# A long convolution before two MoE layers: the first half's spectrum stored frequency by frequency, eight complex sums moved to GpSimd

## The chip, the cores and the metric

The kernel runs on one core of a Trainium2 chip. The metric is the device time of one execution in microseconds (us). The engines are TensorE (PE; its weight loads are shown apart as PEld), VectorE (DVE), ScalarE (ACT), GpSimd (POOL) and SyncE (SP), which here only issues DMAs. Each engine works off its own instructions in order and waits for semaphores of the others.

## What is computed

```python
def _attn_ref(x, v, pos_emb, w1, w2):          # S = 12480, D = 128
    h_mlp = np.maximum(pos_emb @ w1, 0.0) @ w2
    window = np.exp(-0.01 * pos)[:, None]
    u = x * v
    Uf = np.fft.rfft(u, n=2 * S, axis=1)
    Hf = np.fft.rfft(h_mlp * window, n=2 * S, axis=0)
    y = np.fft.irfft(Uf * Hf[None, :, :], n=2 * S, axis=1)[:, :S, :]
    return x * y
# then two MoE layers, 128 -> 2048 -> 128:
# relu(h)^2 and max(h, 0) + alpha * min(h, 0)
```

All operands are float32. The convolution is a multiplication of spectra, over a transform of length 110 x 229 that is done as two smaller ones (a over 110, b over 229), each a set of matmuls with tables of cosines and sines.

## The kernel before

The 128 channels are worked on in two halves of 64 (h = 0, 1). A stage is a Python generator that yields after each step; `run((gen, n), ...)` interleaves generators, advancing each by 1/n per step, and so fixes the order on every engine. The stages around the change are, with their place in the profile:

1. **First transforms** (44.6 to 115.3 us). `u_stage(0)` transforms the first half in 16 steps of four channels (`u_mm_a3`, then `u_mm_b3`), while `r_stage` makes the filter's tiles r. In `u_mm_b3` two DVE operations (line 301) write the even and the odd sums, 448 elements each, into the spectrum's place U(0, ...).
2. **Second transforms with first products** (115.3 to 188.9). `u_stage(1)` does the second half (`u_mm_a`, `u_mm_b`, DVE line 325). `p_stage(0)` multiplies the first half's spectrum by the filter's: 14 items, each for four frequencies. An item has two halves. In a half PE makes the filter's spectrum H in a PSUM bank (line 368: four matmuls, shown as 8 records), and DVE multiplies it with the spectrum into tile A (named T) or B (named wide) (line 373). Then DVE subtracts and adds A and B (line 382, two operations of 512 elements), and `finish` on GpSimd writes sums and differences back over the spectrum (line 352). The last item of all finishes on DVE. Two PSUM banks (ring r_h) hold H.
3. **Second products with first inverse** (200.7 to 250.8). `p_stage(1)` does the same for the second half, while `b_stage(0)` does the inverse b transform of the first half: 16 steps of 8 matmuls (line 391, 16 records a step), whose lhsT is one cell of the spectrum, its 112 values (2 x 56 frequencies); ACT copies the result out (line 399).
4. **Second inverse** (250.8 to 277.7), with the decoding of MoE weights, then the inverse a transform with the output product (`y_stage`, lines 444 and 445, to 333), then the MoE layers to the end.

GpSimd also prepares the input (`prep`, lines 271 and 210), some steps ahead of the transform that reads it; SP loads it (`load`). xv_ring has NV = 10 pairs of buffers for it. The first half's spectrum lies in gaps of the large buffer G, whose rows are 256 floats apart: cell x is a row, and its 112 values are neighbours. The first XF = 16 cells lie in one set of gaps, the rest in another, so that each operation over all cells comes in two parts.

Of the kernel before, what the change touches and what calls it, by code (L numbers as in the profile page):

```python
# [9 lines left out]
F32 = mybir.dt.float32  # L10
# [3 lines left out]
I64 = mybir.dt.int64  # L14
# [7 lines left out]
KA = HA + 1  # L22
# [5 lines left out]
KP = KA // 2  # L28
XF = 16
NAP = -(-NA // 16) * 16  # L30
DH = D // 2
DG = 4
# [26 lines left out]
def kernel(  # L59
# [70 lines left out]

    def U(h, x0, n):
        if h:
            return R2[:HB].rearrange("p (x k) -> p x k", k=K2)[:, x0:x0 + n]
        if x0 < XF:
            return gap[0][:HB, x0:x0 + n, 128 - K2:128]
        return gap[1][:HB, x0 - XF:x0 - XF + n, 0:K2]

    def parts(h):
        return [(0, D)] if h else [(0, XF), (XF, D - XF)]

    NV = 10
    at = [XF]

    def rows(n):
        at[0] += n
        assert at[0] <= HX
        return gap[0][:, at[0] - n:at[0]]

    a_ring = [[rows(DG)[:, :, 0:K2] for _ in range(2)] for _ in range(2)]
    t_ring = [rows(DG)[:, :, 0:K2] if i else gap[1][:, D - XF:D - XF + DG, 0:K2] for i in range(2)]  # L150
    n_old = -(-(HP - at[0]) // DG)
# [137 lines left out]
    def u_mm_b3(k):  # L289
        hi, lo = a_t.pop(k)  # L290
        ps = [bank(r_b, HB, 2, DG, KA) for _ in range(2)]
        t = t_ring[k % 2][:HB].rearrange("p d (c k) -> p c d k", c=2)
        for eo in (1, 0):
            th, tl = (tab[:, eo] for tab in df3)
            for i, (w, x) in enumerate(((th, lo), (tl, hi), (th, hi))):
                nc.tensor.matmul(ps[eo], lhsT=w, rhs=x[:, eo], start=i == 0, stop=i == 2)
            if eo:
                nc.scalar.copy(out=t, in_=ps[1])
        u = U(0, 2 * DG * k, 2 * DG).rearrange("p (d s) (c k) -> p s c d k", s=2, c=2)
        for s, op in enumerate((ALU.add, ALU.subtract)):  # L300
            nc.vector.tensor_tensor(out=u[:, s], in0=ps[0], in1=t, op=op)

# [9 lines left out]
    def u_mm_b(k):  # L312
        h, g = divmod(k, NG)
        a = a_t.pop(k)
        pe = bank(r_b, HB, DG, 2, KA)
        po = bank(r_b, HB, DG, 2, KA)
        nc.tensor.matmul(po[:, :, 0], lhsT=sinb, rhs=a[0][:, :, 1])
        nc.tensor.matmul(pe[:, :, 0], lhsT=cosb, rhs=a[0][:, :, 0])
        nc.tensor.matmul(po[:, :, 1], lhsT=sinb, rhs=a[1][:, :, 0])
        t = t_ring[k % 2][:HB].rearrange("p d (c k) -> p d c k", c=2)  # L320
        nc.scalar.copy(out=t, in_=po)
        nc.tensor.matmul(pe[:, :, 1], lhsT=cosb, rhs=a[1][:, :, 1])
        u = U(h, 2 * DG * g, 2 * DG).rearrange("p (d s) (c k) -> p d s c k", s=2, c=2)
        for s, op in enumerate((ALU.add, ALU.subtract)):
            nc.vector.tensor_tensor(out=u[:, :, s], in0=pe, in1=t, op=op)

    def u_stage(h, parts=None):
        for k in range(h * NG, (h + 1) * NG + 1):
            if k < (h + 1) * NG:
                prep(k + NV - 4)  # L330
                load(k + NV - 1)
                u_mm_a3(k, parts) if parts else u_mm_a(k)
                yield
            if k > h * NG:
                u_mm_b3(k - 1) if parts else u_mm_b(k - 1)
                yield
# [3 lines left out]
    p_order += [(j + nj - 6) % nj for j in range(nj)]  # L340

    def p_stage(h, t_ring, r_ring):
        def at_j(x0, m, j):
            return U(h, x0, m).rearrange("p x (c k) -> p x c k", c=2)[:, :, :, 4 * j:4 * j + 4]

        def finish(n, j, A):
            eng = nc.vector if n == 2 * nj - 1 else nc.gpsimd
            for x0, m in parts(h):
                y = A[:, x0:x0 + m].rearrange("p (d s) c k -> p d s c k", s=2)
                u = at_j(x0, m, j).rearrange("p (d s) c k -> p d s c k", s=2)  # L350
                for s, op in ((0, ALU.add), (1, ALU.subtract)):
                    eng.tensor_tensor(out=u[:, :, s], in0=y[:, :, 0], in1=y[:, :, 1], op=op)

        for n in range(h * nj, (h + 1) * nj):
            j = p_order[n]
            m = p_order[min(n + 2, 2 * nj - 1)]
            if m not in r_t:
                del r_t[p_order[n - 1]]
                r_t[m] = r_ring()
                nc.sync.dma_start(out=r_t[m].rearrange("p q c k -> p (q c k)"), in_=spill[m])  # L360
            r = r_t[j]
            A = t_ring()
            B = wide[:HB].rearrange("p (x c k) -> p x c k", k=4, c=2)
            for c, out_c in enumerate((A, B)):
                H = bank(r_h, HB, DH, 2, 2, 2)
                for q in range(2):
                    for s in range(2):
                        nc.tensor.matmul(
                            H[:, :, s, q], lhsT=r[:, q, 2 * s + c], rhs=w2_sb[:, h * D:(h + 1) * D]
                        )  # L370
                hv = H.rearrange("p d s q r -> p (d s) (q r)")
                for x0, m in parts(h):
                    nc.vector.tensor_tensor(
                        out=out_c[:, x0:x0 + m],
                        in0=at_j(x0, m, j),
                        in1=hv[:, x0:x0 + m].unsqueeze(2).to_broadcast([HB, m, 2, 4]),
                        op=ALU.mult,
                    )
                if c == 0:
                    yield  # L380
            for c, op in ((0, ALU.subtract), (1, ALU.add)):
                nc.vector.tensor_tensor(out=A[:, :, c], in0=A[:, :, c], in1=B[:, :, 1 - c], op=op)
            finish(n, j, A)
            yield

    def b_stage(h, alone):
        for g in range(NG):
            for e in range(2):
                p = bank(r_y if alone else r_ab, K2, DG, HX)
                for d in range(DG):  # L390
                    nc.tensor.matmul(
                        p[:, d], lhsT=U(h, 2 * (g * DG + d) + e, 1)[:, 0], rhs=icosb if e == 0 else isinb
                    )
# [103 lines left out]
    def weights(pool, n=2):  # L497
        s_ring = ring_of(pool, 3, [128, n, 128], I64, "s_w")
        rings = [ring_of(pool, 2, [128, n * 128], F32, t) for t in ("f_w", "m_w")]

# [35 lines left out]

        return go

# [178 lines left out]
    with tc.manual_schedule():  # L717
        with ExitStack() as st:
# [17 lines left out]
            wst = ctx.enter_context(tc.tile_pool(name="wst", bufs=1))  # L736
            decode = weights(wst)
            back = decode([
# [7 lines left out]
            big = st.enter_context(tc.tile_pool(name="tt", bufs=1, side="right"))  # L746
            tt = ring_of(big, 2, [HB, D, 2, 4], F32, "T")
            p0, q0 = p_stage(0, tt, r_ring), p_stage(1, tt, r_ring)
            run((u_stage(1), 2 * NG), (p0, 2 * nj - 4))
            next(back)  # L750
            for _ in range(3):
                next(q0)
            run((q0, 2 * nj + 3), (b_stage(0, False), NG))
        banks = six + last_two("pair", 512, 512)
        r_y.items = six
        wa = ctx.enter_context(tc.tile_pool(name="wa", bufs=1))
        w["i0"] = [(wa.tile([128, 2, NT, 128], F32R, name="w_i0"), 0, NT)]
# [173 lines left out]
```

## Time and profile before

| what | value |
|---|---|
| median of 3 runs | 1404.55 us (1404.37 to 1404.98) |
| profiled execution | 1402.77 us of device time, span of its core 1401.0 us |
| PE busy | 1389.3 us, 99% |
| DVE, ACT, POOL busy | 1158.4, 977.8, 1006.9 us |
| mean granted PE clock | 0.998 of 2.4 GHz |

A busy share of PE counts its records from start to end, and records of successive matmuls overlap; how fast PE really goes is read from the starts of successive records. Stages are told apart by their windows, and what ends a wait stands in brackets behind a row of the timeline.

### The profile page before, as it was taken

To read this page: it belongs to the slowest core of one execution; us is meant where nothing else is said; L and a number is where in the kernel's file an instruction comes from. 1 tells how busy PE (TensorE), PEld (TensorE's weight loads), DVE (VectorE), ACT (ScalarE), POOL (GpSimd) and SP (SyncE) were. 2 spreads that over 40 slices of the span, in tenths; PEclk is the share of its full clock that TensorE was granted. 3 is DMA by queue.
4 is the path that set the end of the run, shared out by engine and by line. 5 is a ranking of instruction groups with operands and counts; after the bars stand their busy time and mean duration, and the time that the engine had idled before them with its cause. 6 is when DMAs were issued, how large, how long until landed. Compare 5 with 4: busy or idle time off the path is not lost.

```text
span 1401.0 us, 22648 instructions
## 1 busy us (share of the span) xinstructions
PE 1389.3 (99%) x7566; PEld 1205.7 (86%) x7566; DVE 1158.4 (83%) x1824; ACT 977.8 (70%) x1850; POOL 1006.9 (72%) x841
## 2 busy tenths in 40 slices
PE   9999999999999999999999999999999999999998
PEld 9999989998888888888888888888888888888898
DVE  5688899786888888888888888788888878888888
ACT  4454322725988778778777877877787787777777
POOL 4954856446787777877777777777777777777777
PEclk9999999999999999999999999999999999999999
DMA  7565323397000000000000000000000000000000
GB/s 209 173 200 177 94 82 109 105 275 218 24 16 1 8 1 9 8 8 8 9 8 0 9 8 9 8 8 8 8 2 8 8 9 8 9 8 1 8 9 19
DMA packets 59016, 66.20 MB, mean 47 GB/s; under 512 B 6226, under 2 KB 48019, under 8 KB 58771
## 3 DMA queue, kind: packets, MB, share of 16 engines
q1 hardware_dynamic: 57802, 60.62, 14.3%
q0 software_dynamic: 688, 3.93, 0.8%
q8 instruction: 59, 0.97, 0.3%
q14 instruction: 58, 0.48, 0.1%
q10 hardware_dynamic: 409, 0.21, 0.1%
HBM read 47.83 MB, written 16.92 MB: 46 GB/s over the span
## 4 chain that ended last, share of the span: by engine, by line
PE 79%; ACT 1%; POOL 1%; DVE 1%; issue 0%; POOLq 0%; DVEq 0%
PE bank L605 19%; PE bank L607 19%; PE bank L606 19%; PE pair L606 6%; PE pair L607 6%; PE pair L605 6%; PE bank L444 2%; PE bank L445 2%; ACT G L399 1%; POOL g L658 1%; ACT pair L517 0%; ACT w_i L487 0%; DVE pair L477 0%; DVE f_w L481 0%; DVE pair L475 0%
## 5 line engine op out<-in xcount | busy, mean ns | idle before, releaser
L658 POOL TENSOR_TENSOR g<-R,g 128x512 fp32r<-128x512 f32 (+1 forms) x601 | 779.4, 1314 | 253.5 <-ACT g L647 241.3
L640 DVE SCALAR_TENSOR_TENSOR R<-bank,e 128x512 f32<-128x512 f32 (+1 forms) x800 | 530.1, 672 | 137.4 <-POOL g L658 99.8
L647 ACT CAST g<-R 128x512 fp32r<-128x512 f32 (+1 forms) x800 | 469.8, 605 | 77.5 <-DVE R L640 70.0
L625 ACT ACTIVATE e<-bank 128x512 f32<-128x512 f32 (+1 forms) x400 | 235.0, 587 | 106.6 <-PE bank L607 104.6
L630 DVE TENSOR_SCALAR e<-bank,alpha 128x512 f32<-128x512 f32 (+1 forms) x266 | 195.0, 733 | 36.0 <-PE bank L607 34.4
L658 DVE TENSOR_TENSOR g<-R,g 128x512 fp32r<-128x512 f32 (+1 forms) x199 | 184.7, 928 | 0.0
L606 PE MATMUL pair<-g,w_o 128*128 128x512 f32 (+1 forms) x400 | 153.7, 384 | 0.4 <-POOL g L658 0.4
L605 PE MATMUL bank<-x,w_i 128*128 128x512 f32 (+1 forms) x400 | 153.8, 384 | 0.0
L605 PE MATMUL pair<-g,w_o 128*128 128x512 f32 (+1 forms) x400 | 153.6, 384 | 0.0
L606 PE MATMUL bank<-x,w_i 128*128 128x512 f32 (+1 forms) x400 | 153.6, 384 | 0.0
L607 PE MATMUL bank<-x,w_i 128*128 128x512 f32 (+1 forms) x400 | 153.5, 384 | 0.0
L607 PE MATMUL pair<-g,w_o 128*128 128x512 f32 (+1 forms) x400 | 153.5, 384 | 0.0
L605 PE MATMUL bank<-g,w_o0b 128*128 128x512 f32 (+1 forms) x350 | 134.4, 384 | 0.0
L606 PE MATMUL bank<-g,w_o0b 128*128 128x512 f32 (+1 forms) x350 | 134.3, 384 | 0.0
L607 PE MATMUL bank<-g,w_o0b 128*128 128x512 f32 (+1 forms) x350 | 134.3, 384 | 0.0
L627 ACT ACTIVATE e<-bank 128x512 f32<-128x512 f32 (+1 forms) x134 | 78.7, 588 | 33.5 <-PE bank L607 32.9
L628 ACT ACTIVATE e<-e,alpha 128x512 f32<-128x512 f32 (+1 forms) x134 | 95.5, 713 | 4.4
L605 PEld LDWEIGHTS bank<-x,w_i 128*128 128x128 f32 x400 | 75.1, 188 | 15.0 <-DVE R L640 0.9
L606 PEld LDWEIGHTS pair<-g,w_o 128*128 128x128 f32 x400 | 75.2, 188 | 14.8 <-POOL g L658 1.0
L607 PEld LDWEIGHTS bank<-x,w_i 128*128 128x128 f32 x400 | 75.1, 188 | 14.4
L607 PEld LDWEIGHTS pair<-g,w_o 128*128 128x128 f32 x400 | 75.1, 188 | 14.4
L606 PEld LDWEIGHTS bank<-x,w_i 128*128 128x128 f32 x400 | 75.2, 188 | 13.8
(137 smaller groups left out, 2526.0 us busy)
## 6 DMA issues: line engine op xcount, KB each, us to landing
r<-spill SPq DMA_DIRECT2D x22, 460.0 KB, 3.2
G<-in_xs_dram SPq DMA_DIRECT2D x32, 224.0 KB, 3.5
G<-in_vs_dram SPq DMA_DIRECT2D x32, 224.0 KB, 3.5
spill<-r SPq DMA_DIRECT2D x14, 460.0 KB, 3.0
out_dram<-R SPq DMA_DIRECT2D x23, 256.0 KB, 2.0
R<-in_xt_dram SPq DMA_DIRECT2D x27, 218.0 KB, 4.2
s_w<-in_moe_w_in_dram SPq DMA_DIRECT2D x16, 256.0 KB, 3.6
s_w<-in_moe_w_out_dram SPq DMA_DIRECT2D x16, 256.0 KB, 2.7
```

Source lines behind the costliest of these rows:

```text
L444: nc.tensor.matmul(pv, lhsT=le, rhs=re, start=True, stop=False)
L445: nc.tensor.matmul(pv, lhsT=lo, rhs=ro, start=False, stop=True)
L605: nc.tensor.matmul(p, lhsT=wl, rhs=xh, start=first, stop=False)
L606: nc.tensor.matmul(p, lhsT=wh, rhs=xl, start=False, stop=False)
L607: nc.tensor.matmul(p, lhsT=wh, rhs=xh, start=False, stop=last)
L625: nc.scalar.activation(out=r, in_=p, func=ACTF.Relu)
L627: nc.scalar.activation(out=r, in_=p, func=ACTF.Relu, scale=-1.0)
L628: nc.scalar.activation(out=r, in_=r, func=ACTF.Copy, scale=alpha[:, t:t + 1])
L630: nc.vector.tensor_scalar(out=r, in0=p, scalar1=0.0, scalar2=alpha[:, t:t + 1], op0=ALU.min, op1=ALU.mult)
L640: nc.vector.scalar_tensor_tensor(out=g, in0=p, scalar=0.0, in1=r, op0=ALU.max, op1=op)
L647: nc.scalar.copy(out=gh, in_=g)
L658: eng.tensor_tensor(out=gl, in0=g, in1=gh.bitcast(F32), op=ALU.subtract)
```

## The change

The first half's spectrum is turned: a row of the gap now holds one of the 112 values (a frequency, real or imaginary) for all 128 cells, `u0[p, c, k, s, d]`, with the d index running through neighbours; one value of the next frequency lies 256 floats, that is 1,024 bytes, further. All of it fits one set of gaps, so the split in two parts goes. `u_mm_b3` writes it with k as the innermost loop; `b_stage` takes a column of it as lhsT (`u_cells`). In the first products tiles A and B are laid out in the same way, and H is written into its bank with an order (q r s d) in place of (d s q r).

For the 8 items n of `on_pool`, of 28, GpSimd does the two sums of line 382 too; B of such an item is a tile of the T ring, which has three tiles in place of two. The space comes from two gaps that become free and from the decoding of weights, whose later tiles are now set up after the products. xv_ring has 12 pairs, so signals are loaded two steps earlier; they are prepared as far ahead as before. The pace of `p_stage(0)` is 29 steps in place of 24, against the transforms' 32, and two steps of the second products follow in place of three.

```diff
     gap = [G.rearrange("p (n h x) -> p n h x", h=2, x=128)[:, :, h] for h in range(2)]
 
-    def U(h, x0, n):
+    u0 = gap[1][:HB, :K2].rearrange("p (c k) (s d) -> p c k s d", c=2, s=2)
+    u1 = R2[:HB].rearrange("p (d s c k) -> p d s c k", s=2, c=2, k=KA)
+
+    def u_cells(h, d, e):
         if h:
-            return R2[:HB].rearrange("p (x k) -> p x k", k=K2)[:, x0:x0 + n]
-        if x0 < XF:
-            return gap[0][:HB, x0:x0 + n, 128 - K2:128]
-        return gap[1][:HB, x0 - XF:x0 - XF + n, 0:K2]
-
-    def parts(h):
-        return [(0, D)] if h else [(0, XF), (XF, D - XF)]
-
-    NV = 10
-    at = [XF]
+            return u1[:, d, e].rearrange("p c k -> p (c k)")
+        return gap[1][:HB, :K2, e * DH + d]
+
+    NV = 12
+    at = [0]
...
                 nc.tensor.matmul(ps[eo], lhsT=w, rhs=x[:, eo], start=i == 0, stop=i == 2)
             if eo:
                 nc.scalar.copy(out=t, in_=ps[1])
-        u = U(0, 2 * DG * k, 2 * DG).rearrange("p (d s) (c k) -> p s c d k", s=2, c=2)
         for s, op in enumerate((ALU.add, ALU.subtract)):
-            nc.vector.tensor_tensor(out=u[:, s], in0=ps[0], in1=t, op=op)
+            u = u0[:, :, :, s, DG * k:DG * (k + 1)].rearrange("p c k d -> p c d k")
+            nc.vector.tensor_tensor(out=u, in0=ps[0], in1=t, op=op)
 
     def u_mm_a(k):
...
@@ -320,14 +317,13 @@
         t = t_ring[k % 2][:HB].rearrange("p d (c k) -> p d c k", c=2)
         nc.scalar.copy(out=t, in_=po)
         nc.tensor.matmul(pe[:, :, 1], lhsT=cosb, rhs=a[1][:, :, 1])
-        u = U(h, 2 * DG * g, 2 * DG).rearrange("p (d s) (c k) -> p d s c k", s=2, c=2)
         for s, op in enumerate((ALU.add, ALU.subtract)):
-            nc.vector.tensor_tensor(out=u[:, :, s], in0=pe, in1=t, op=op)
+            nc.vector.tensor_tensor(out=u1[:, DG * g:DG * (g + 1), s], in0=pe, in1=t, op=op)
 
     def u_stage(h, parts=None):
         for k in range(h * NG, (h + 1) * NG + 1):
             if k < (h + 1) * NG:
-                prep(k + NV - 4)
+                prep(k + NV - 6)
                 load(k + NV - 1)
...
+    on_pool = {1, 4, 7, 10, 15, 18, 21, 24}
+
     def p_stage(h, t_ring, r_ring):
-        def at_j(x0, m, j):
-            return U(h, x0, m).rearrange("p x (c k) -> p x c k", c=2)[:, :, :, 4 * j:4 * j + 4]
+        def shaped(t):
+            if h:
+                return t.rearrange("p (d s c k) -> p c (d s) k", s=2, c=2, k=4)
+            return t.rearrange("p (c k x) -> p c k x", c=2, k=4)
+
+        def at_j(j):
+            k = slice(4 * j, 4 * j + 4)
+            if h:
+                return u1[:, :, :, :, k].rearrange("p d s c k -> p c (d s) k")
+            return u0[:, :, k].rearrange("p c k s d -> p c k (s d)")
 
         def finish(n, j, A):
             eng = nc.vector if n == 2 * nj - 1 else nc.gpsimd
-            for x0, m in parts(h):
-                y = A[:, x0:x0 + m].rearrange("p (d s) c k -> p d s c k", s=2)
-                u = at_j(x0, m, j).rearrange("p (d s) c k -> p d s c k", s=2)
-                for s, op in ((0, ALU.add), (1, ALU.subtract)):
-                    eng.tensor_tensor(out=u[:, :, s], in0=y[:, :, 0], in1=y[:, :, 1], op=op)
+            if h:
+                y, u = A.rearrange("p (d s z) -> p s d z", s=2, z=8), u1[:, :, :, :, 4 * j:4 * j + 4]
+                u = [u[:, :, s] for s in range(2)]
+            else:
+                y = A.rearrange("p (z s d) -> p s z d", s=2, z=8)
+                u = [u0[:, :, 4 * j:4 * j + 4, s] for s in range(2)]
+            for s, op in ((0, ALU.add), (1, ALU.subtract)):
+                eng.tensor_tensor(out=u[s], in0=y[:, 0], in1=y[:, 1], op=op)
 
...
+            apart = n in on_pool
+            B = t_ring() if apart else wide[:HB]
             A = t_ring()
-            B = wide[:HB].rearrange("p (x c k) -> p x c k", k=4, c=2)
             for c, out_c in enumerate((A, B)):
-                H = bank(r_h, HB, DH, 2, 2, 2)
+                H = r_h()[:HB].rearrange("p (d s q r) -> p s q d r" if h else "p (q r s d) -> p s q d r", s=2, q=2, r=2)
                 for q in range(2):
                     for s in range(2):
-                        nc.tensor.matmul(
-                            H[:, :, s, q], lhsT=r[:, q, 2 * s + c], rhs=w2_sb[:, h * D:(h + 1) * D]
-                        )
-                hv = H.rearrange("p d s q r -> p (d s) (q r)")
-                for x0, m in parts(h):
-                    nc.vector.tensor_tensor(
-                        out=out_c[:, x0:x0 + m],
-                        in0=at_j(x0, m, j),
-                        in1=hv[:, x0:x0 + m].unsqueeze(2).to_broadcast([HB, m, 2, 4]),
-                        op=ALU.mult,
-                    )
+                        nc.tensor.matmul(H[:, s, q], lhsT=r[:, q, 2 * s + c], rhs=w2_sb[:, h * D:(h + 1) * D])
+                hv = H.rearrange("p s q d r -> p (d s) (q r)" if h else "p s q d r -> p (q r) (s d)")
+                o, u = shaped(out_c), at_j(j)
+                if h:
+                    o, u = (x.rearrange("p c x k -> p x c k") for x in (o, u))
+                    hv = hv.unsqueeze(2).to_broadcast([HB, D, 2, 4])
+                else:
+                    hv = hv.unsqueeze(1).to_broadcast([HB, 2, 4, D])
+                nc.vector.tensor_tensor(out=o, in0=u, in1=hv, op=ALU.mult)
                 if c == 0:
                     yield
+            a, b = shaped(A), shaped(B)
             for c, op in ((0, ALU.subtract), (1, ALU.add)):
-                nc.vector.tensor_tensor(out=A[:, :, c], in0=A[:, :, c], in1=B[:, :, 1 - c], op=op)
+                eng = nc.gpsimd if apart else nc.vector
+                eng.tensor_tensor(out=a[:, c], in0=a[:, c], in1=b[:, 1 - c], op=op)
             finish(n, j, A)
             yield
...
                 for d in range(DG):
                     nc.tensor.matmul(
-                        p[:, d], lhsT=U(h, 2 * (g * DG + d) + e, 1)[:, 0], rhs=icosb if e == 0 else isinb
+                        p[:, d], lhsT=u_cells(h, g * DG + d, e), rhs=icosb if e == 0 else isinb
                     )
                 dst = gv[:, :, e, h * DH + g * DG:h * DH + (g + 1) * DG]
...
@@ -744,15 +758,18 @@
             (wide,) = last_two("wide", 1024)
             r_b.items, r_h.items, r_ab.items = six[2:4], six[4:6], six[0:4]
             big = st.enter_context(tc.tile_pool(name="tt", bufs=1, side="right"))
-            tt = ring_of(big, 2, [HB, D, 2, 4], F32, "T")
+            tt = ring_of(big, 2, [HB, D * 8], F32, "T")
+            third = st.enter_context(tc.tile_pool(name="third", bufs=1))
+            tt.items.append(third.tile([HB, D * 8], F32, name="T2"))
             p0, q0 = p_stage(0, tt, r_ring), p_stage(1, tt, r_ring)
-            run((u_stage(1), 2 * NG), (p0, 2 * nj - 4))
+            run((u_stage(1), 2 * NG), (p0, 2 * nj + 1))
             next(back)
-            for _ in range(3):
+            for _ in range(2):
```


On PE this is the end of the second transforms and the beginning of the first inverse. L314 to L322 are transforms, L368 (before) and L378 (after) halves of products, L391 and L401 the inverse. First before, then of the changed kernel:

```order
L319 MATMUL bank_72<-G,dfb 115x4x56
L322 MATMUL bank_71<-G,dfb 115x4x56
L368 MATMUL bank_73<-w_sb,r_100 115x64x2 x4
L368 MATMUL bank_74<-w_sb,r_100 115x64x2 x4
L368 MATMUL bank_73<-w_sb,r_98 115x64x2 x4
L368 MATMUL bank_74<-w_sb,r_98 115x64x2 x4
L368 MATMUL bank_73<-w_sb,r_99 115x64x2 x4
L368 MATMUL bank_74<-w_sb,r_99 115x64x2 x4
L368 MATMUL bank_73<-w_sb,r_100 115x64x2 x4
L368 MATMUL bank_74<-w_sb,r_100 115x64x2 x4
L391 MATMUL bank_69<-dfb,G 112x116 x4
```


```order
L314 MATMUL bank_72<-G,dfb 115x4x56
L315 MATMUL bank_71<-G,dfb 115x4x56
L316 MATMUL bank_72<-G,dfb 115x4x56
L319 MATMUL bank_71<-G,dfb 115x4x56
L378 MATMUL bank_73<-w_sb,r_99 115x64x2 x4
L378 MATMUL bank_74<-w_sb,r_99 115x64x2 x4
L378 MATMUL bank_73<-w_sb,r_100 115x64x2 x4
L401 MATMUL bank_69<-dfb,G 112x116 x4
```


Eight halves of products stood between the last transform and the inverse, and three do now; the five others have moved ahead, between the transforms.

On DVE this is a stretch of the first products among the second transforms (L325, L321), before and after; T and wide are the tiles A and B, G the spectrum:

```order
L325 TENSOR_TENSOR R_82<-bank_71,G 115x4x112 x2
L373 TENSOR_TENSOR T_1089<-G,bank_73 115x128
L373 TENSOR_TENSOR T_1089<-G,bank_73 115x896
L373 TENSOR_TENSOR wide_1084<-G,bank_74 115x128
L373 TENSOR_TENSOR wide_1084<-G,bank_74 115x896
L382 TENSOR_TENSOR T_1089<-T_1089,wide_1084 115x128x4 x2
L325 TENSOR_TENSOR R_82<-bank_71,G 115x4x112 x2
L373 TENSOR_TENSOR T_1088<-G,bank_73 115x128
L373 TENSOR_TENSOR T_1088<-G,bank_73 115x896
L325 TENSOR_TENSOR R_82<-bank_71,G 115x4x112 x2
```


```order
L386 TENSOR_TENSOR T_1088<-G,bank_73 115x1024
L386 TENSOR_TENSOR wide_1083<-G,bank_74 115x1024
L392 TENSOR_TENSOR T_1088<-T_1088,wide_1083 115x512 x2
L321 TENSOR_TENSOR R_82<-bank_71,G 115x4x112 x2
L386 TENSOR_TENSOR T_1087<-G,bank_73 115x1024
L386 TENSOR_TENSOR T_1092<-G,bank_74 115x1024
L321 TENSOR_TENSOR R_82<-bank_71,G 115x4x112 x2
L386 TENSOR_TENSOR T_1088<-G,bank_73 115x1024
L321 TENSOR_TENSOR R_82<-bank_71,G 115x4x112 x2
L386 TENSOR_TENSOR wide_1083<-G,bank_74 115x1024
```


Each product is one instruction in place of two, and an item on GpSimd (its B in a T tile too) has no sums (L382, L392) behind its products. On GpSimd the sums stand in front of that item's `finish`, between two preparations (L268, L207):

```order
L361 TENSOR_TENSOR G<-T_1087 115x2x4x64 x2
L268 TENSOR_TENSOR G<-G 110x4x115
L207 TENSOR_TENSOR G<-G,sig_sb 110x4x115
L392 TENSOR_TENSOR T_1092<-T_1092,T_1088 115x512 x2
L361 TENSOR_TENSOR G<-T_1092 115x2x4x64 x2
```


## Rows read from the trace of the kernel before

**Rows 1.** Windows by stage: length, busy per engine (records), clock, DMA, GB/s

```profile
core 0: us, PE busy (x) PEld busy (x) DVE busy (x) ACT busy (x) POOL busy (x), PEclk, DMA share, GB/s
44.60:115.30 70.70, 70.26 (x578) 67.72 (x577) 57.81 (x120) 35.34 (x77) 45.19 (x39) 1.00 0.64 192
115.30:188.90 73.60, 73.34 (x594) 71.49 (x592) 64.04 (x106) 25.87 (x49) 49.10 (x62) 1.00 0.42 129
188.90:200.70 11.80, 8.88 (x50) 8.02 (x50) 11.56 (x18) 0.00 (x0) 7.86 (x11) 0.71 0.12 39
200.70:250.80 50.10, 49.12 (x451) 47.02 (x450) 48.27 (x55) 16.93 (x31) 32.29 (x26) 1.00 0.35 103
```

**Rows 2.** Timeline of PE, one step: start, length (us), line, records

```profile
176.12 1.77 PE L309 MATMUL bank<-dfa,G 110*115 110x112 f32 x16
...
179.25 1.04 PE L368 MATMUL bank<-w_sb,r 128*115 128x128 f32 x8
180.12 1.77 PE L309 MATMUL bank<-dfa,G 110*115 110x112 f32 x16
```

**Rows 3.** Timeline of PE at the hand-over, [idle before <- releaser]

```profile
187.03 1.91 PE L368 MATMUL bank<-w_sb,r 128*115 128x128 f32 x16
190.71 1.13 PE L368 MATMUL bank<-w_sb,r 128*115 128x128 f32 x8 [1.77 <-DVE T L373]
...
194.56 6.28 PE L368 MATMUL bank<-w_sb,r 128*115 128x128 f32 x32 [0.91 <-DVE T L373]
200.68 1.75 PE L391 MATMUL bank<-dfb,G 115*112 115x116 f32 x16
```

**Rows 4.** Timeline of PE, second products with first inverse

```profile
217.87 1.75 PE L391 MATMUL bank<-dfb,G 115*112 115x116 f32 x16
219.46 2.17 PE L368 MATMUL bank<-w_sb,r 128*115 128x128 f32 x16
...
225.24 1.75 PE L391 MATMUL bank<-dfb,G 115*112 115x116 f32 x16
```

**Rows 5.** Lines of DVE by form, 40 to 255: busy, mean ns, idle before

```profile
L382 DVE TENSOR_TENSOR T<-T,wide 115x512 f32<-115x512 f32 x56 | 36.0, 683 | 1.0
L301 DVE TENSOR_TENSOR G<-bank,G 115x448 f32<-115x448 f32 x32 | 18.5, 619 | 3.6 <-PE bank L296 2.8 <-ACT G L298 0.5
L373 DVE TENSOR_TENSOR wide<-R,bank 115x1024 f32<-115x1024 f32 x14 | 17.2, 1226 | 0.7 <-PE bank L368 0.2
L373 DVE TENSOR_TENSOR T<-R,bank 115x1024 f32<-115x1024 f32 x14 | 17.0, 1212 | 0.0
L373 DVE TENSOR_TENSOR wide<-G,bank 115x896 f32<-115x896 f32 x14 | 15.3, 1095 | 0.5
L373 DVE TENSOR_TENSOR wide<-G,bank 115x128 f32<-115x128 f32 x14 | 4.0, 289 | 3.6 <-PE bank L368 3.6
```

**Rows 6.** Lines of POOL by form, same stretch

```profile
L352 POOL TENSOR_TENSOR R<-T 115x512 f32<-115x512 f32 x26 | 32.3, 1264 | 15.5 <-DVE T L382 15.5
```

**Rows 7.** Source line 197: ns min/median/max, first and last start, forms

```profile
L197 DVE SCALAR_TENSOR_TENSOR G<-bank,win_sb x9: 262/1056/1073, 5.6 to 17.7; 110x512 f32<-110x512 f32 x7, 110x256 f32<-110x256 f32 x1, 110x64 f32<-110x64 f32 x1
```

**Rows 8.** Timeline of PE, last steps of the first transforms

```profile
114.14 0.47 PE L296 MATMUL bank<-xl,df 115*115 115x448 f32 x1 [0.44 <-DVE G L301]
```

**Rows 9.** Timeline of PE's weight loads, two stretches

```profile
110.44 0.97 PEld L242 LDWEIGHTS pair<-dfb,R 115*128 115x128 f32 x8
...
278.89 0.31 PEld L445 LDWEIGHTS bank<-ido,G 112*128 112x128 f32 x2
279.13 0.31 PEld L444 LDWEIGHTS bank<-ide,G 112*128 112x128 f32 x2
279.37 0.31 PEld L445 LDWEIGHTS bank<-ido,G 112*128 112x128 f32 x2
```

**Rows 10.** Timeline of PE in the MoE layers

```profile
799.73 0.39 PE L605 MATMUL bank<-x,w_i 128*128 128x512 f32 x1
...
802.90 0.39 PE L607 MATMUL bank<-x,w_i 128*128 128x512 f32 x1
```

More of the change, by code (lines that the diff above doesn't have):

```diff
@@ L28 @@
 KP = KA // 2
-XF = 16
 NAP = -(-NA // 16) * 16
@@ L149 @@
     a_ring = [[rows(DG)[:, :, 0:K2] for _ in range(2)] for _ in range(2)]
-    t_ring = [rows(DG)[:, :, 0:K2] if i else gap[1][:, D - XF:D - XF + DG, 0:K2] for i in range(2)]
+    t_ring = [rows(DG)[:, :, 0:K2] if i else gap[1][:, K2:K2 + DG, 0:K2] for i in range(2)]
     n_old = -(-(HP - at[0]) // DG)
@@ L312, in u_mm_b @@
     def u_mm_b(k):
-        h, g = divmod(k, NG)
+        g = k - NG
         a = a_t.pop(k)
@@ L497, in weights, with more @@
     def weights(pool, n=2):
-        s_ring = ring_of(pool, 3, [128, n, 128], I64, "s_w")
-        rings = [ring_of(pool, 2, [128, n * 128], F32, t) for t in ("f_w", "m_w")]
+        s_ring = ring_of(pool, 2, [128, n, 128], I64, "s_w")
+        rings = []
+        def more(pool):
+            s_ring.items.append(pool.tile([128, n, 128], I64, name="s_w2"))
+            rings.extend(ring_of(pool, 2, [128, n * 128], F32, t) for t in ("f_w", "m_w"))
         def go(todo):
@@ L535, in go @@
                     yield
-        return go
+        return go, more
     def in_place(key):
@@ L736 @@
             wst = ctx.enter_context(tc.tile_pool(name="wst", bufs=1))
-            decode = weights(wst)
+            decode, more = weights(wst)
             back = decode([
@@ L755 @@
         r_y.items = six
+        more(ctx.enter_context(tc.tile_pool(name="wst2", bufs=1)))
         wa = ctx.enter_context(tc.tile_pool(name="wa", bufs=1))
```

## Prediction

> **What bounds the kernel now.** I read the windows by stage first [rows 1], then PE's timeline inside each, then the groups of instructions by shape. In both transform stages and in the second products TensorE (PE) shows 98% busy or more, so a busy share does not separate them; the pace does. In the second transform stage PE repeats a cycle without gaps [rows 2]: the transforms of one step run from 176.12 to 179.25, 3.13 us, and a half of products (8 records of line 368) from 179.25 to 180.12, 0.87 us. From 115.3 to the last transform's end at 187.03 there are 16 steps and 23 halves: 16 x 3.13 + 23 x 0.87 = 70.1 of 71.7 us. That stage is PE's, and only 1.6 us of it is stall.
>
> Then comes a gap [rows 3]: from 187.03 to 200.68, 13.65 us, PE has only 8 halves, 7.0 us of work at that pace. It waits for VectorE's (DVE's) products, and the granted clock falls: 0.71 over 188.9 to 200.7 [rows 1], that is, partly the lower level of 1.2 GHz. So 6.65 us are lost. In the stage after it two products and two inverse steps repeat every 7.37 us (217.87 to 225.24) [rows 4]. PE's own work in that is 2 x 1.59 for 32 inverse records (16 from 217.87 to 219.46, so 99 ns each) and 4 x 0.87 for products: 6.66. DVE, busy 48.27 of 50.1 us [rows 1], sets this period. Over the stage PE has 24 halves (20.9) and 256 inverse records (25.4): 46.3 of 50.1, 3.8 us lost.
>
> All that the change can win on PE's side is thus 1.6 + 6.65 + 3.8 = 12 us, 0.9% of the time. What follows (second inverse, outputs, both MoE layers) starts when the first inverse ends, so a shift of that end (250.8) moves the kernel's end one for one.
>
> **What it takes off.** *DVE.* Each first-half product is one instruction of 1,024 elements in place of 128 + 896. The second half has that size already: 1,226 ns against 289 + 1,095 for tile B [rows 5]. That is 0.16 us a product, 4.4 us over 28. Eight items give their two sums of 683 ns to GpSimd: 10.9 us in all, half in each stage. In the second stage DVE then has at most 14 x 2.44 for products, 10 x 1.37 for sums and 32 x 0.62 for line 325 (the shape of line 301): 67.7 us under PE's 74.5 (below). In the third it has 14 x 2.44 + 10 x 1.37 = 47.9.
>
> *GpSimd.* It gets 16 sums; the nearest row is its own 512-element operation at 1,264 ns [rows 6]: 10 us a stage. It was busy 49.1 of 73.6 us in the second stage [rows 1] and gets 5 more for two finishing items that fell behind it: 64 of 75. It is fullest while it still prepares signals; the third tile gives DVE about two items (over 10 us) before a tile comes back, so I take 0 and keep 1 us of stall for the range. The signal loads that move ahead on SP's queue keep their distance to the preparations: nothing, since DMA is 42% busy there.
>
> *The hand-over.* The order shows 3 halves behind the last transform in place of 8. PE's work ahead of that point is 16 x 3.13 + 28 x 0.87 = 74.5, with the stalls of today 76.1. After it PE fills two banks (1.75 us) and needs the first one back. DVE still has one product, two sums, two line-325 pairs and the next product behind it, some 6.1 us after PE's last first-half product, against 3.1 + 1.75 on PE: 1.3 us of waiting, then 0.87 for the third half. The inverse's first matmul also waits for GpSimd's last finish (2 x 1.26 after DVE's sums), which is over by then.
>
> **What it adds.** *Writes of line 301.* They now step through 1,024 bytes between elements (frequency is the inner loop). The only strided writer of today is line 197, 920 bytes apart: 512 elements take 1,056 ns, 64 take 262 [rows 7], so 1.772 ns an element and 149 fixed. For 448 that makes 943 in place of 619 ns [rows 5]: 32 x 0.324 = 10.4 us more on DVE in the first stage, where it is busy 57.8 of 70.7 and PE 70.3 [rows 1]. It still fits (68.2), and a freed bank is wanted only a step later, except at the end, where PE already waits for this line [rows 8]: the last pair is 0.65 us longer. I take 0.65; ends 0 (the writes cost as now) and 3 (DVE's queue becomes the bound).
>
> *Weight loads of the first inverse.* This is the term that decides. Its 256 records take as lhsT one column of the frequency rows: 112 elements 1,024 bytes apart, where they were neighbours. The records now follow at 99 ns, which is what their 116 moving columns need (128 of line 368 take 0.87 / 8 = 109), so any longer load shows in full. No row has such a load. From below: line 444 loads 128 columns 8 bytes apart, line 242 128 neighbours; two loads of 444/445 take 0.235 us (278.89, 279.13, 279.37), 118 ns each, while 8 of line 242 take 0.97 with 0.19 for the last, 111 each [rows 9]. So a small stride already costs some 7 ns, and below that nothing: 99. From above: line 197's price for a lone element, 1.772 ns [rows 7]. I take it, because the 8-byte row sits where it puts that load: if 1.772 is the price of one access that can bring two such neighbours, 64 x 1.772 = 113 of the 118 are explained and 5 are a fixed part; a load that pays by columns alone would have shown 111. Lone columns then make 112 x 1.772 + 5 = 204 ns.
>
> The Trainium skill (SBUF — State Buffer, section Door 1: The DMA port swizzle) says that SBUF has lines of 16 bytes, and that each access that crosses into a new line pays. The trace agrees: MoE matmuls read 512 neighbours, 128 such lines, and start 226 ns apart (14 in 3.17 us) [rows 10], which is 128 x 1.77. By that page too a load of 112 lone columns would be an estimated 198 ns and more, with the sum as below.
>
> **Sum**, in the profiled execution's time (span 1401.0, device time 1402.77; the runs' median is 1404.55, 1.78 above). First stage +0.65. Last transform ends at 115.3 + 0.65 + 76.1 = 192.1; with 1.75 + 1.3 + 0.87 the inverse starts at 196.0 in place of 200.7: -4.7, the 0.65 included. Third stage: 25 halves x 0.87 + 256 x 0.204 = 21.8 + 52.2 = 74.0 in place of 50.1: +23.9; DVE's 47.9 lies under it. Together +19.2: 1422.0 in the profile's terms, **1424** as a median.
>
> **Rivals.**
> 1. *Strided loads are free* (the other side). The third stage is then 21.8 + 25.4 = 47.2, DVE about equal, 1 us of stall: 48.2, -1.9; with -4.7 that is -6.6: **1398**. For it: DVE's price is of writes, and a read may be fetched ahead; against it: the 118 of rows 9. It decides below 99 + 6.6/256 = 125 ns a record; above that the kernel is slower. The Trainium skill (TensorE: Matmul & The Clock Gate, section LDWEIGHTS) counts a load by columns alone, columns / 1.2; by that estimate 112 need 93 ns at any stride and this rival holds. The trace speaks against it with 118 and 111 for the same 128 columns.
> 2. *The clock falls.* With loads of 204 ns the array streams under half of the time of an inverse record. Today the granted clock fell after 188.94 to 192.05, when PE ran one half, and the 32 records from 194.56 took 6.1 us in place of 3.5 [rows 3]. At the lower level a half costs 0.87 more; if half of the 25 do: +11, **1435**; all: 1446. Against it: products, dense, stand between the inverse steps.
> 3. *First products slow down in PSUM.* Line 368 now writes neighbours in order 512 bytes apart; today it writes pairs 32 bytes apart, at the same 109 ns a record as its 128 columns need [rows 2], so nothing is the near end. If lone words cost as on line 197 (1.7 times), 28 x 0.87 x 0.7 = 17 us: **1441**. The same section of the skill gives PSUM lines of 8 bytes and says that matmuls slow down on patterns that are not contiguous; today's pairs fill such a line, which is why no row tests it.
>
> **How the numbers follow.** Forecast 0.76, rival 1 0.13, rival 2 0.06, rival 3 0.05. The low end, 1411, is a load halfway between its ends (151 ns, 256 x 0.052 = 13.4 us over rival 1); the high end, 1438, takes in half of the clock's case and 3 us for line 301. Outside lie rival 1 and most of rival 3. No change means within 0.2% (2.8 us), about what a measurement of this kernel can tell: faster 0.12, same 0.02, slower 0.86.
>
> **What will show it.** PEld of the first inverse: 204 ns from start to start against 99, with no DVE wait between; line 301 at 943 ns; the inverse starting at 196 and ending at 270. Right on the other parts and wrong on the sum would be: inverse records still at 99 and an end at 244 (rival 1), a granted clock under 1 after 196 (rival 2), halves longer than 0.87 between 115 and 192 (rival 3). A T tile waited for by DVE on GpSimd would show the third tile too small.

## The result, and the profile after

The changed kernel takes 1421.93 us (median of 4 runs, 1420.35 to 1422.32), the kernel before 1404.46 (4 runs, 1402.86 to 1404.98). The ratio is 1.0125, 95% interval 1.0113 to 1.0138: 17.5 us slower. The profiled execution took 1420.35 us, with a span of 1418.6.

The windows by stage of the changed kernel, cut where its stages change (first transforms, second transforms with first products, hand-over, second products with first inverse, second inverse):

```profile
core 0: us, PE busy (x) PEld busy (x) DVE busy (x) ACT busy (x) POOL busy (x), PEclk, DMA share, GB/s
44.60:116.00 71.40, 70.44 (x579) 67.90 (x578) 62.83 (x120) 35.52 (x78) 45.15 (x39) 1.00 0.64 191
116.00:192.80 76.80, 75.24 (x610) 73.15 (x609) 63.88 (x80) 25.50 (x49) 62.90 (x52) 1.00 0.37 111
192.80:197.30 4.50, 4.50 (x27) 4.28 (x25) 3.31 (x4) 0.35 (x1) 0.17 (x1) 0.66 0.02 4
197.30:268.10 70.80, 70.80 (x458) 70.80 (x456) 45.11 (x49) 16.94 (x31) 42.37 (x34) 1.00 0.27 79
268.10:295.20 27.10, 25.71 (x259) 25.53 (x258) 21.47 (x51) 21.86 (x53) 14.60 (x20) 1.00 0.36 100
```

Against [rows 1] the inverse starts at 197.3 in place of 200.7, a gain of 3.4 us. The next stage then takes 70.8 us in place of 50.1. DVE, which was its limit with 48.27 us of 50.1, is now busy 45.11 of 70.8; PE and its weight loads fill the window. Behind it nothing changes: the second inverse takes 27.1 us (26.9 before), and the rest follows 17.5 us later than before.

PE's timeline in that stage (start, length, line, records), which answers to [rows 4]:

```profile
228.33 1.91 PE L378 MATMUL bank<-w_sb,r 128*115 128x128 f32 x16
230.08 3.24 PE L401 MATMUL bank<-dfb,G 115*112 115x116 f32 x16
233.15 1.91 PE L378 MATMUL bank<-w_sb,r 128*115 128x128 f32 x16
```

Sixteen records of the inverse run from 230.08 to 233.15, 3.07 us or 192 ns each, where they took 99. Sixteen of the product take 1.75 us, 109 ns each, as before. No row has an idle time in front. The source view of the inverse's line (first inverse from G, second from R) has the cause on the weight loads: durations min/median/max in ns, first and last start.

```profile
L401 PEld LDWEIGHTS bank<-dfb,G x256: 264/287/288, 197.2 to 267.9; 115*112 115x112 f32 x128
...
L401 PEld LDWEIGHTS bank<-dfb,R x256: 177/177/192, 268.1 to 293.4; 115*112 115x112 f32 x128
```

The same 115 x 112 load takes 110 ns longer from start to end where its columns lie 1,024 bytes apart; loads overlap, so from start to start it is 93 (192 against 99). The line that writes the turned spectrum (301 before, 298 now) and DVE's products by form, with the idle time before them and what ended it:

```profile
L298 DVE TENSOR_TENSOR G<-bank,G 115x448 f32<-115x448 f32 x32 | 27.8, 945 | 3.5 <-PE bank L293 2.7 <-ACT G L295 0.5
...
L386 DVE TENSOR_TENSOR T<-G,bank 115x1024 f32<-115x1024 f32 x18 | 21.8, 1215 | 6.1 <-POOL G L361 3.9 <-POOL G L268 1.2 <-PE bank L378 0.7
```

945 ns in place of 619 [rows 5]. At the end of the first transforms PE waits longer for that line (answers to [rows 8]):

```profile
114.82 0.46 PE L293 MATMUL bank<-xl,df 115*115 115x448 f32 x1 [0.96 <-DVE G L298]
```

The row of line 386 has a wait that was not there: DVE stands 5.1 us for GpSimd before its products. At the hand-over (answers to [rows 3]) PE's timeline is:

```profile
191.52 0.64 PE L315 MATMUL bank<-G,dfb 115*115 115x224 f32 x2 [1.27 <-DVE R L321]
...
193.02 4.41 PE L378 MATMUL bank<-w_sb,r 128*115 128x128 f32 x24
197.27 3.03 PE L401 MATMUL bank<-dfb,G 115*112 115x116 f32 x15
```

Three halves, 24 records, take 4.25 us to the inverse's start, 2.6 at the full clock: the granted clock was 0.66 in that window.

### The profile page after: what moved, and what is told of

It reads as the page before. It is cut to its first block, busy times and chain, and to the rows that moved or that the text cites. A ratio compares the mean times of both kernels' runs of the same rounds, so it can differ in the third digit from the quotient of the medians.

```text
span 1418.6 us, 22573 instructions
## 1 busy us (share of the span) xinstructions
PE 1408.8 (99%) x7566; PEld 1227.6 (87%) x7566; DVE 1153.0 (81%) x1780; ACT 978.2 (69%) x1850; POOL 1023.1 (72%) x829
## 4 chain that ended last, share of the span: by engine, by line
PE 78%; ACT 1%; POOL 1%; DVE 1%; issue 0%; POOLq 0%; DVEq 0%
PE bank L619 19%; PE bank L620 19%; PE bank L621 19%; PE pair L620 6%; PE pair L619 6%; PE pair L621 6%; PE bank L454 2%; PE bank L455 2%; ACT G L409 1%; POOL g L672 1%; ACT pair L531 0%; ACT w_i L497 0%; DVE pair L487 0%; DVE f_w L491 0%; DVE pair L485 0%
```

## The experiments

The theory behind all of them: the loss is the lone columns of the first inverse's weight loads (columns without a neighbour that is read too), and a load pays for each group of 16 bytes that it touches. The rivals: the turned layout costs elsewhere (writes, PSUM, clock), or the price has another form. A second question came with the numbers: which part of the change brings the 3.4 us, and what it would bring without the loads.

**Neighbours as weights, in the changed kernel.** The inverse takes 112 neighbours of a row, so it reads other values than those of its cell, and the first half of the convolution is not computed; all else is as changed.

```diff
-        return gap[1][:HB, :K2, e * DH + d]
+        return gap[1][:HB, (e * DH + d) % K2, 0:K2]
```

> The changed kernel, but the first inverse takes as lhsT 112 neighbours of one row of the spectrum in place of one column of it. So it multiplies other values (the first half of the convolution is not computed); number, shape and order of all instructions are kept. Theory (the loads of lone columns are the whole loss): inverse records back from 193 to 99 ns, the third stage some 48 us in place of 70.8, first inverse over near 245, 1399 us. Rival (the loss lies in the new order, the sums on GpSimd or the PSUM layout of the first products): third stage stays near 70, 1420 or more.

Measured: 1398.35 us (1396.77 to 1399.7), ratio to before 0.9962 [0.995, 0.9974]. PE's timeline:

```profile
228.30 1.91 PE L378 MATMUL bank<-w_sb,r 128*115 128x128 f32 x16
230.05 1.75 PE L401 MATMUL bank<-dfb,G 115*112 115x116 f32 x16
```

The stage takes 47.7 us. The distance between the elements of one operand gives 1421.93 - 1398.35 = 23.6 us (22.9 by the two ratios to the kernel before), the stage alone 23.1, and 256 records at 93 ns are 23.8. So the loads are the whole loss, and the other parts of the change together gain about 5 us.

**Lone columns as weights, in the kernel before.** The opposite edit, in the first inverse alone.

```diff
+    def cells(h, x):
+        if h:
+            return U(h, x, 1)[:, 0]
+        return gap[1][:HB, :K2, x % K2]
...
-                        p[:, d], lhsT=U(h, 2 * (g * DG + d) + e, 1)[:, 0], rhs=icosb if e == 0 else isinb
+                        p[:, d], lhsT=cells(h, 2 * (g * DG + d) + e), rhs=icosb if e == 0 else isinb
```

> The kernel before, but the first inverse takes as lhsT a column across its rows, 112 elements 1,024 bytes apart (other values; the first half of the convolution is not computed); nothing else is touched. Theory: records go from 99 to 193 ns, the third stage becomes PE's: 24 x 0.87 + 256 x 0.193 = 70.3 in place of 50.1, so 1424 to 1425 us. Rival: the stage is set by VectorE and hides part of it; under 1415 us.

Measured: 1424.39 us, ratio 1.0149 [1.0135, 1.0163]. PE's timeline has 192 ns a record (229.26 to 232.33), and the stage takes 70.0 us in place of 50.1:

```profile
229.26 3.23 PE L396 MATMUL bank<-dfb,G 115*112 115x116 f32 x16
232.33 1.91 PE L368 MATMUL bank<-w_sb,r 128*115 128x128 f32 x16
```

Nothing else of the layout is needed to make the loss.

**The price by step.** The second inverse of the kernel before, each of its steps with another distance between columns.

```diff
+    STRIDES = [1, 1, 2, 2, 3, 3, 4, 4, 5, 6, 8, 16, 32, 64, 128, 1]
...
+        x0, s = 4 * (x % 32), STRIDES[g]
+        return R2[:HB, x0:x0 + (K2 - 1) * s + 1:s]
```

> The kernel before, but step g of the second inverse (16 steps of 16 records) takes as lhsT 112 elements of the spectrum at a step of 1, 1, 2, 2, 3, 3, 4, 4, 5, 6, 8, 16, 32, 64, 128, 1 floats (other values; the second half of the convolution is not computed). Price of a record by step. Theory (an access brings a group of 16 bytes, and each new group costs about two columns' time): 99 ns at 1, 99 to 104 at 2, some 145 to 150 at 3 (three of four elements open a group), 193 from 4 on and no more up to 128. Rival 1 (only a step of 16 bytes or more pays, whatever groups are touched): 3 as 2, then a jump to 193 at 4. Rival 2 (distance counts): it goes on rising from 4 to 128.

One run, 1418.73 us. Windows of PE, cut where the first record of each distance starts: distances 1, 2, 3 and 4 with 32 records each, then 5, 6, 8, 16, 32, 64 and 128 with 16 (the count in a row also holds records that reach in from outside).

```profile
core 0: us, PE busy (x), PEclk, DMA share, GB/s
251.53:254.70 3.17, 3.17 (x34) 1.00 0.00 0
254.70:258.01 3.31, 3.31 (x34) 1.00 0.15 25
258.01:262.91 4.90, 4.90 (x34) 1.00 0.43 122
262.91:269.47 6.56, 6.56 (x34) 1.00 0.33 101
269.47:272.58 3.11, 3.11 (x18) 1.00 0.32 84
272.58:275.70 3.12, 3.12 (x17) 1.00 0.02 5
275.70:279.05 3.35, 3.35 (x17) 1.00 0.27 78
279.05:282.11 3.06, 3.06 (x17) 1.00 0.30 86
282.11:285.19 3.08, 3.08 (x17) 1.00 0.26 85
285.19:288.27 3.08, 3.08 (x18) 1.00 0.00 0
288.27:291.34 3.07, 3.07 (x17) 1.00 0.25 85
```

Length by records: 99 ns at distance 1, 103 at 2, 153 at 3, 205 at 4, 194 and 195 at 5 and 6, 209 at 8, 191 to 193 from 16 on. In groups of 16 bytes 112 columns touch 28, 56, 84 and then always 112: 153 / 84 and 205 / 112 are 1.82 and 1.83 ns, 103 / 56 is 1.84, and from 16 on it is 1.71 to 1.72. At that price the 28 of distance 1 would make 51 ns, less than the 99 of the moving columns. The step at 3 speaks against a threshold between neighbours and all others, the flat row from 16 to 128 against a price that grows with distance. That 4 and 8 are dearer than 5, 6 and all from 16 on is open.

**All but the layout.** The kernel before, with the sums on GpSimd, the third tile, the pace of 29, two steps of the second products ahead in place of three and the weights' tiles set up later, in the old layout. The signals' buffers stay at `NV = 10`. Core of the edit:

```diff
+            apart = n in on_pool
+            B = t_ring() if apart else wide[:HB].rearrange("p (x c k) -> p x c k", k=4, c=2)
...
-            run((u_stage(1), 2 * NG), (p0, 2 * nj - 4))
+            run((u_stage(1), 2 * NG), (p0, 2 * nj + 1))
             next(back)
-            for _ in range(3):
+            for _ in range(2):
```

> The kernel before with all of the change but the layout: the spectrum, its products in two parts and NV = 10 stay; eight items' sums on GpSimd, the third tile, the pace of 29, two steps ahead, and weights' tiles later are taken over. Theory (the layout alone loses, the rest wins): hand-over as in the changed kernel, inverse records at 99 ns, third stage near 48, first inverse over near 245: 1398 to 1400 us. Rival (the rest needs the shorter products of the layout, VectorE sets the second transform stage): 1402 or more.

Measured: 1401.59 us (1400.4 to 1402.02), ratio 0.9983 [0.9974, 0.9991]: a gain, but a smaller one than forecast. DVE's waits between 115 and 196 us (line waited for, total us, times, longest) say where it stayed:

```profile
DVE T L376 <- POOL G L354: 5.4, 4, 1.9
```

DVE waits for a T tile that GpSimd still holds, and the last record of the transforms starts 79.0 us after the stage's first matmul, against 76.5 in the changed kernel. The third stage takes 47.4 us, as forecast.

**Sums later.** The same, with six items in place of eight, none before the tenth.

```diff
-    on_pool = {1, 4, 7, 10, 15, 18, 21, 24}
+    on_pool = {9, 11, 15, 18, 21, 24}
```

> All of the change but the layout, with the first half's sums on GpSimd for items 9 and 11 alone, when the preparations are over (n = 9, 11, 15, 18, 21, 24). Theory: no wait of VectorE for GpSimd in the second transform stage, last transform at 192 to 193 in place of 195.0, 1399 to 1400 us. Rival (without the layout VectorE sets that stage, 74 us of work): last transform at 195 or later, 1401.6 or more.

Measured: 1399.16 us (1398.22 to 1400.32), ratio 0.9961 [0.9949, 0.9974]. The last record of the transforms starts at 76.7. So the early sums on GpSimd cost the kernel above 2.3 us in that stage.

**The pace alone.** The kernel before with nothing but the two numbers of the pace.

```diff
-            run((u_stage(1), 2 * NG), (p0, 2 * nj - 4))
+            run((u_stage(1), 2 * NG), (p0, 2 * nj + 1))
...
-            for _ in range(3):
+            for _ in range(2):
```

> The kernel before with one part of the change: the first products' pace of 29 in place of 24, and two steps of the second products ahead in place of three. Theory (the gap at the hand-over was mostly the products left over): it goes, the inverse starts near 197 in place of 200.7; the third stage keeps its 50.1 us, which VectorE sets; 1400 to 1401 us. Rival (VectorE's total sets the hand-over, and the pace only moves the gap): the inverse starts near 200, 1403 or more.

Measured: 1399.85 us (1398.14 to 1400.97), ratio 0.9963 [0.9949, 0.9976]. PE's timeline at the hand-over, and its windows for the third stage and for the output products (columns as in the windows of the changed kernel):

```profile
193.09 1.91 PE L368 MATMUL bank<-w_sb,r 128*115 128x128 f32 x16
196.09 1.13 PE L368 MATMUL bank<-w_sb,r 128*115 128x128 f32 x8 [1.08 <-DVE T L373]
197.05 1.75 PE L391 MATMUL bank<-dfb,G 115*112 115x116 f32 x16
```

```profile
197.10:246.30 49.20, 49.20 (x458) 47.68 (x457) 48.59 (x57) 16.90 (x31) 32.30 (x26) 1.00 0.36 107
273.30:329.00 55.70, 55.69 (x459) 55.69 (x460) 43.52 (x100) 10.21 (x28) 21.63 (x29) 0.97 0.86 250
```

The inverse starts 3.6 us earlier than in [rows 3] without a sum on GpSimd or a turned layout. In the third stage DVE is still nearly full: 48.59 of 49.2 us.

**Second-half sums only, in the changed kernel.** `on_pool = {15, 18, 21, 24}`, to see what DVE's 5.1 us of waits cost.

> The changed kernel with sums on GpSimd in the second half alone (n = 15, 18, 21, 24); the first half's are VectorE's again. Theory (in the second transform stage GpSimd, which still prepares signals, is late with the sums, and VectorE waits for a T tile): VectorE's waits for GpSimd there, 5.1 us and more in the changed kernel, go; the last transform ends 1.5 to 2.5 us earlier than 192.8, the kernel takes some 1420. Rival (VectorE needs the relief): its 5.1 us come back on the path and the last transform ends no earlier; 1422 or more.

Measured: 1421.69 us, ratio 1.012 [1.0106, 1.0134]. DVE's waits for GpSimd are gone from that stage, and the last record of the transforms starts 76.4 us after the stage's first matmul against 76.5, so not earlier by more than 0.1 us. PE's idle time in the stage is the same with and without them: 0.29 us for ACT and 1.27 for DVE's line 321, both in the last step. My theory that they cost time falls: they were off the path, which was PE's.

**Runs of four in the write.** The changed kernel, with line 298 writing runs of four neighbours and reading lone elements of its two operands instead.

```diff
-            u = u0[:, :, :, s, DG * k:DG * (k + 1)].rearrange("p c k d -> p c d k")
-            nc.vector.tensor_tensor(out=u, in0=ps[0], in1=t, op=op)
+            u = u0[:, :, :, s, DG * k:DG * (k + 1)]
+            x, y = (z.rearrange("p c d k -> p c k d") for z in (ps[0], t))
+            nc.vector.tensor_tensor(out=u, in0=x, in1=y, op=op)
```

> The changed kernel with the loops of line 298 exchanged: it writes runs of four neighbours and reads PSUM and the ScalarE copy in steps of 224 bytes. Theory (a write pays by groups of 16 bytes, a read of one operand the same): the write falls to 619 ns, but the strided read of the copy in SBUF keeps it near 943. Rival (only writes pay): near 619. Whole kernel within 1 us of the changed one in either case.

One run, 1420.98 us. The expectation had the copy's distance wrong: PSUM is read 224 bytes apart, the copy, whose rows lie in a gap, 1,024. The line in its source view (ns min/median/max):

```profile
L299 DVE TENSOR_TENSOR G<-bank,G x32: 899/946/961, 51.4 to 117.4; 115x448 f32<-115x448 f32 x32
```

946 ns, as before the edit (948). If runs of four are cheap to write, reading lone elements costs DVE what writing them does. For the condition there is a row of the changed kernel, at another distance: line 361 writes runs of four 224 bytes apart, and its 512 elements take 689 ns, as the 684 of line 392.

```profile
L361 DVE TENSOR_TENSOR R<-T x2: 685/689/693, 262.1 to 262.7; 115x512 f32<-115x512 f32 x2
L392 DVE TENSOR_TENSOR T<-T,wide x40: 680/684/689, 122.6 to 261.4; 115x512 f32<-115x512 f32 x40
```

That runs 1,024 bytes apart are as cheap to write, no run shows, and which of the two operands read sets the price was not parted.

**Pace, and the sums of the second half.** The kernel in the old layout, third tile kept, with `on_pool = {15, 18, 21, 24}`.

> The kernel before with the pace and the two steps ahead, and the sums on GpSimd over the third tile in the second half alone (n = 15, 18, 21, 24); no layout. Theory (the first half's sums bring nothing, the second half's take VectorE off the third stage): last transform and start of the inverse as with the pace alone (76.7 us after the stage's first matmul), third stage 47.3 us in place of 49.1: 1398 to 1399. Rival (two sums of the first half count too): 1400 or more.

Measured: 1397.65 us (1396.64 to 1398.08), ratio 0.9951 [0.9939, 0.9964], the fastest of all. Its window of the third stage:

```profile
198.00:245.40 47.40, 47.40 (x458) 47.37 (x457) 44.38 (x49) 16.90 (x31) 42.17 (x34) 1.00 0.39 118
```

DVE is down to 44.38 us, PE's own work bounds the stage, and 1.8 us go against the pace alone (49.2 to 47.4). The intervals of the two kernels' ratios overlap, so the runs alone do not part them.

**Sums without the pace.** The kernel with all but the layout, with the old pace (`2 * nj - 4`, three steps).

> The kernel before with the eight items' sums on GpSimd over the third tile, at the old pace of 24 and with three steps ahead; no layout. Theory (the gap at the hand-over comes of the pace, the third stage of the sums): 8 halves behind the last transform and the inverse's start near 200 as before, third stage 47 to 48 in place of 50.1: 1401.5 to 1403. Rival (less work on VectorE closes the gap by itself): the inverse starts 3 us earlier, 1399 or less.

Measured: 1404.53 us (1402.64 to 1406.39), ratio 1.0002 [0.9993, 1.0012]. The windows of the gap and of the third stage:

```profile
187.70:201.30 13.60, 8.71 (x67) 7.50 (x66) 13.39 (x21) 0.53 (x1) 8.91 (x13) 1.00 0.12 36
201.30:251.20 49.90, 48.16 (x451) 46.78 (x450) 43.67 (x47) 16.90 (x31) 42.17 (x34) 1.00 0.32 97
```

The gap is as long as before, and the third stage, from which I wanted 47 to 48 us, takes 49.9 though DVE is busy only 43.67 of it. Products left over from the gap are not what keeps it long, for DVE stands idle in the stage: four times, 11 us apart, it waits 1.0 us for a bank from PE, and PE then 0.43 us for DVE's product. Two of the four on DVE's timeline, then on PE's:

```profile
206.38 1.23 DVE L376 TENSOR_TENSOR wide<-R,bank 115x1024 f32<-115x1024 f32 x1 [1.01 <-PE bank L371]
217.34 1.23 DVE L376 TENSOR_TENSOR wide<-R,bank 115x1024 f32<-115x1024 f32 x1 [1.00 <-PE bank L371]
```

```profile
210.12 1.13 PE L371 MATMUL bank<-w_sb,r 128*115 128x128 f32 x8 [0.43 <-DVE T L376]
221.07 1.13 PE L371 MATMUL bank<-w_sb,r 128*115 128x128 f32 x8 [0.43 <-DVE T L376]
```

The kernel with all but the layout differs from this one in the two numbers of the pace alone, and its third stage takes 47.4 us with no such wait of PE. So the two numbers set the order of the third stage as well, and the sums on GpSimd shorten that stage only with them.

## Why the prediction was right

**Weight loads of the first inverse: right in mechanism, 12 ns too dear.** The forecast took 204 ns a record; it was 192. Over 256 records that is 3.1 us, and the stage took 70.8 where the sum has 74.0. This is the mis-sized term; against it the inverse started 1.3 us later than forecast, and the two together are the 2 us by which 1424 lies above 1421.93. The price of line 197 with 5 ns on top is 1.82 ns a column; that is what distances 3 and 4 cost for each group of 16 bytes, while at 1,024 bytes a column costs 1.72. That TensorE's loads pay about what DVE's writes do was an assumption, and no row of the kernel before could test it at this distance; that it came within 6% is shown by the runs alone. The reading of [rows 9], one access for two neighbours 8 bytes apart, is borne out by the 103 ns at distance 2. The agreement seen in [rows 10] is none: 226 ns for 512 moving neighbours are 0.44 ns a column, near one cycle at 2.4 GHz (0.42), so a count of columns gives it as well as a count of lines. The rule of the Trainium skill (SBUF — State Buffer, section Door 1: The DMA port swizzle) of lines of 16 bytes holds for these loads: the price follows the count of such lines up to distance 4 and not the distance after. That a stride of up to 4 fp32 is free, as the Trainium skill says in the same place, does not hold for them: distance 3 costs 153 ns and distance 4 205, against 99.

**Rival 1, free loads: refuted.** It needed under 125 ns a record, and 192 were measured. Its sum for all the rest stands: 1398, where the changed kernel with neighbours took 1398.35. The count by columns alone (the Trainium skill, TensorE: Matmul & The Clock Gate, section LDWEIGHTS) does not hold here: one and the same 112 columns take from 99 to 209 ns.

**Line 301: right in its time, too high in DVE's sum.** 943 ns forecast, 945 measured, and the first stage is 0.7 us longer where 0.65 was taken; the rest lay under PE. But DVE's busy time there rose to 62.8 us and not to 68.2. Records of successive DVE operations overlap, as the row of line 298 shows: 32 of 945 ns would be 30.2 us, and it is busy 27.8. So a sum of durations overstates DVE's load; the same goes for its 47.9 us in the third stage, where 45.1 were measured.

**Hand-over: right in kind, 1.3 us late.** The inverse started at 197.3 against 196.0. The three halves before it started at 193.0 against 192.1: the sum kept the stalls of the kernel before, and in the changed one PE waits 1.27 us for DVE inside the last transform (0.26 before). From there it took 4.25 us in place of 3.9, without the forecast wait of 1.3 us, because in this execution the clock fell and the 24 records filled the time. The changed kernel with neighbours, whose instructions up to here are the same, kept a clock of 1.00. It shows the wait, 1.08 us, and takes 3.96:

```profile
193.51 1.91 PE L378 MATMUL bank<-w_sb,r 128*115 128x128 f32 x16
196.51 1.13 PE L378 MATMUL bank<-w_sb,r 128*115 128x128 f32 x8 [1.08 <-DVE T L386]
197.47 1.75 PE L401 MATMUL bank<-dfb,G 115*112 115x116 f32 x16
```

So the fall cost 0.3 us. It does not make the gap of the kernel before either: the kernel before with lone columns as weights passed that gap at 1.00 in 13.4 us, against 13.65 in [rows 3].

**GpSimd: wrong, without effect.** I took 0 and kept 1 us of stall; DVE waited 5.1 us, though GpSimd's busy time was as forecast (62.9 us against 64). It cost nothing in the changed kernel, whose PE was the limit, and 2.3 us in the old layout (79.0 against 76.7). The products there are 0.16 us longer each, which may be why; no run tells.

**Rival 2, the clock: no.** 1.00 over the whole third stage. **Rival 3, PSUM: no.** A half of products still takes 0.87 us, with neighbours 512 bytes apart. The lines of 8 bytes that this rival takes from the Trainium skill stand in the section on Door 1 of its page SBUF — State Buffer, not under LDWEIGHTS; that matmuls slow down on patterns that are not contiguous does not show here.

**What each part is worth.** The pace brings 0.37% of the ratio (about 5 us). Sums of the second half bring some 2 us more in the third stage, and only with the new pace; sums of the first half bring nothing or a loss. The loads of the turned layout cost 23 to 24 us. What else comes with the layout and the earlier loading of signals shortens the second transform stage by 2.5 us (76.5 against 79.0) with eight sums on GpSimd; without the early sums the old layout comes to 76.7 as well. In terms of the prediction: its 4.7 us for the hand-over need none of the edits but two numbers.

## What to carry to other kernels

Before a layout is turned for one reader's sake, list all who read it, TensorE's weight loads too: count the 16-byte groups that a load touches, and where their number times 1.8 ns (the price of this case's fp32 loads) exceeds the time of the moving columns, the difference is paid per matmul. Where a change has several parts, price each alone and with the others: here two numbers of the schedule carried nearly all of the gain, and the largest edit all of the loss. A wait that a change adds, even one of 5 us, costs nothing while another engine sets the pace; once that slack goes it costs, here 2.3 us of 5.4.

## What was not expected of the hardware

- A load of 112 lone columns is dearest at distances of 4 and 8 floats (205 and 209 ns) and cheaper beyond (191 to 195).
- DVE operations of 448 elements that read lone elements, from PSUM and SBUF at once, and write runs of four take what those take that write lone elements: 946 against 948 ns.
- At the start of the output products PE idles 1.35 to 1.8 us for ACT, and in five of the kernels (neighbours as weights, all but the layout, pace alone, second-half sums only, sums without the pace) the granted clock then fell to its lower level for some 3.4 us, while in others with the same idle time it did not. In the kernel with the pace alone pairs of records grew from 0.40 to 0.63 us:

```profile
275.05 0.40 PE L445 MATMUL bank<-ido,G 112*128 112x110 f32 x2
...
275.68 0.63 PE L445 MATMUL bank<-ido,G 112*128 112x110 f32 x2
```

With the fall that stage takes 55.7 or 55.8 us, without it 54.2, so 1.6 us are given back. The five are kernels whose hand-over ran at a clock of 1.00; the before and changed kernels, sums later, runs of four and pace with second-half sums had the fall at the hand-over and none here, and lone columns in the kernel before had it at neither place. What decides it is open, with one profile of each kernel.
